# An interleaved attention and Fourier network on one core: when the output projection of the attention layers starts, and how its rows are spread over the steps

## The chip, the cores and the metric

The kernel runs on one core of a Trainium2 chip. The metric is the device time of one execution in microseconds. The core has a matrix engine (PE, with its weight loads PEld), a vector engine (DVE), a scalar engine (ACT), a general engine (POOL) and an engine that issues transfers (SP). Each works through its own instructions in order and waits on semaphores for the others.

## The reference

The input has 2048 rows of 640 numbers. Four layers follow each other: attention, Fourier, attention, Fourier. Each adds its result to its input. The change touches the attention layers alone.

```python
def _A_ref(x, wqkv, wo):
    B, S, D = x.shape
    H = 32; Dh = D // H; W = 256
    qkv = (lambda x, *d: x.transpose(*d))((x @ wqkv).reshape(B, S, 3, H, Dh), 2, 0, 3, 1, 4)
    q, k, v = qkv[0], qkv[1], qkv[2]
    scores = jnp.einsum("bhqd,bhkd->bhqk", q, k) * (Dh ** -0.5)
    idx = jnp.arange(S)
    mask = (idx[:, None] - idx[None, :] >= 0) & (idx[:, None] - idx[None, :] < W)
    scores = jnp.where(mask[None, None], scores, -1e9)
    p = _softmax(scores, axis=-1)
    o = jnp.einsum("bhqk,bhkd->bhqd", p, v)
    return (lambda x, *d: x.transpose(*d))(o, 0, 2, 1, 3).reshape(B, S, D) @ wo

def _B_ref(x, dft_seq_re, dft_seq_im, dft_hid_re, dft_hid_im):
    a = jnp.einsum("bsd,ed->bse", x, dft_hid_re)
    b = jnp.einsum("bsd,ed->bse", x, dft_hid_im)
    y = jnp.einsum("ts,bse->bte", dft_seq_re, a) - jnp.einsum("ts,bse->bte", dft_seq_im, b)
    return y

x = A_x
x = x + _A_ref(_layernorm(x, axis=-1), A_wqkv, A_wo)
x = x + _B_ref(_layernorm(x, axis=-1), B_dft_seq_re, B_dft_seq_im, B_dft_hid_re, B_dft_hid_im)
x = x + _A_ref(_layernorm(x, axis=-1), A_wqkv, A_wo)
x = x + _B_ref(_layernorm(x, axis=-1), B_dft_seq_re, B_dft_seq_im, B_dft_hid_re, B_dft_hid_im)
```

## The kernel before

Products that need full precision split each operand into a rounded high part and the rest (`split`, `cut_job`), and add three products, high by high, high by low and low by high.

**The heads.** An attention layer treats its 32 heads as 8 quads of four. A quad has 16 blocks of 128 rows, so `heads` walks through 128 steps. In step t PE computes the scores of one key block for four heads in two halves (`t_pair`, L657), ACT takes their exponential (`t_exp`, L667), POOL masks it (L673, L677), and one step later PE multiplies the probabilities with the values (`pv`, L692). Ten steps ahead, for unit s = t + 10, PE computes the same scores the other way round (`s_head`, L629), DVE adds a mask and takes the row maxima (L634). Every four steps the maxima are transposed (`m_rows`, L642), ACT writes them to the tile mt, and a transfer on SP (qp<-mt, L647) puts them into two rows of the query tile, where the scores of two to five blocks later need them. So the step t = 16 q + 2 needs the maxima that step t - 4 made.

**The fill.** Between the two halves of a step `fill` gives PE a few matmuls of other work. First this is the projection to queries and keys (`project`, `pieces`): ten chunks of 128 columns (c = 0 to 9, of which 2 to 9 are filled in), each over four quarters of the sequence (sb = 0 to 3), two quarters at a time. Two matmuls on 64 rows each run beside each other (`lockstep`, L255), first one half of the rows, then the other; such a piece pair has 60 matmuls and takes eight steps at the rate of four pairs a step. Its result goes through ACT and POOL to a tile c and with a transfer (qk_d<-c, L522) to memory. `pack` reads it back, for each quad and quarter in twelve transfers, three a step (qp<-qk_d, kp<-qk_d, L592). The list `due` tells at which s a quarter of a quad is packed and how much of the projection must be done by then.

**The output projection.** When the projection is through, `fill` goes on with `partials`: the 16 blocks of output rows, four to a quarter. The inner dimension of 640 is cut into five operand chunks that `CHUNKS` lists by heads: chunks 0 and 1 need heads 0 to 15 (quads 0 to 3), chunk 2 heads 16 to 23, chunk 3 heads 24 to 31, chunk 4 all. A row takes the chunks 0, 1 and 2 early (`EARLY` is 3), 36 matmuls of 64 by 320, with the residual input added on DVE (L975, `y_part`), and the chunks 3 and 4 late (`late`), 12 whole matmuls (L237), after the last heads. `load_y` loads the residual rows (big<-x, L949), four at once at the end of the projection and then one a row. `load_o` loads an operand chunk (x<-o_d, L857) and, once for chunks 0 and 1 together, the reciprocal sums (rr<-r_d, L863); POOL scales (L890), ACT and DVE cut. `prepare` loads and cuts the weights wo and starts the first operand set, at the last projection chunk. `LATE` is the number of matmul pairs in a fill of this phase: 9 for half a row, so a row takes two steps. `after_heads` does the last early rows, the late rows, and the first units of the Fourier layer (L1380).

In the timeline of before, step 92 starts at 413.15 us, step 97 at 426.39, step 98 at 431.97, step 99 at 436.86, step 118 at 500.77, step 125 at 521.74 and step 127 at 526.41; in the second attention layer step 97 starts at 1516.08.

## Time and profile before

| what | value |
|---|---|
| median of 3 runs | 2202.13 us (2198.74 to 2204.55) |
| profiled execution | 2201.15 us, span 2199.4 us |
| PE busy | 2127.3 us, 97% |
| DVE busy | 1620.9 us, 74% |
| ACT busy | 1139.1 us, 52% |
| POOL busy | 969.0 us, 44% |
| transfers | 392.09 MB, mean 178 GB/s |

Busy shares hide two things here. A matmul that waits inside PE's pipeline counts as busy, so the length of a step says more than its busy share. And the losses of one attention layer sit in some 110 us, the steps 92 to 127, and come twice. A view by stretches shows them. "PE banks L657 <- DMA qp<-mt" reads: PE's instruction of line 657, which writes the tile banks, waited for the landing of the transfer that writes qp from mt. Rows of SP give the time of an issue, not of a transfer.

### The profile page before, as it was taken

Reading aid. Unit: us, or ns where it says so; the run is one execution under the profiler, and the core shown is the slowest. Engines: PE = TensorE matmul, PEld = TensorE weight load, DVE = VectorE, ACT = ScalarE, POOL = GpSimd, SP = SyncE. Lnnn points to the kernel's source line nnn. Section 1 sums busy time; section 2 is a strip of 40 time slices with the busy share of each in tenths; the row PEclk is TensorE's granted clock in tenths of the full one; section 3 lists DMA queues with packets and bytes.
Section 4 is the critical chain, followed back from the end, with each engine's and each line's share of the span. In section 5 each row is a group of like instructions: output and inputs, shape, how many; then the busy total and the mean of one; then the engine's idle time right before and its main releaser. Section 6 shows DMA issues by size and latency. Waiting matters only on the chain.

```text
span 2199.4 us, 48840 instructions
## 1 busy us (share of the span) xinstructions
PE 2127.3 (97%) x17872; PEld 1785.7 (81%) x17872; DVE 1620.9 (74%) x3949; ACT 1139.1 (52%) x2125; POOL 969.0 (44%) x1568
## 2 busy tenths in 40 slices
PE   7999999998999999999999999999999999999999
PEld 7987777677868888889999777776777788888899
DVE  6358888786897868776661688887868968687776
ACT  3117776656554545552431377676655545455332
POOL 3037776765513223232330477677655133231324
PEclk9999999999999999999999999999999999999999
DMA  5556656785435453665646466668753354546643
GB/s 182 175 162 186 201 181 207 224 221 164 161 122 171 138 185 127 221 199 194 208 146 188 149 199 183 201 195 231 216 170 135 128 187 135 166 152 207 226 161 127
DMA packets 220175, 392.09 MB, mean 178 GB/s; under 512 B 39200, under 2 KB 85792, under 8 KB 219936
## 3 DMA queue, kind: packets, MB, share of 16 engines
q1 hardware_dynamic: 219936, 388.98, 56.4%
q8 instruction: 141, 2.31, 0.4%
q14 instruction: 98, 0.80, 0.1%
HBM read 273.94 MB, written 113.77 MB: 176 GB/s over the span
## 4 chain that ended last, share of the span: by engine, by line
PE 79%; DVE 7%; ACT 4%; DMA 4%; POOL 3%; issue 3%; SPq 0%; ACTq 0%; DVEq 0%; POOLq 0%
PE banks L1380 29%; PE banks L237 15%; PE banks L255 13%; PE banks L692 6%; PE banks L657 5%; PE banks L1668 5%; PE banks L629 4%; DVE banks L634 1%; DMA qp<-qk_d 1%; DVE qp L230 1%; ACT pt L667 1%; DMA qk_d<-c 1%; PE banks L339 1%; POOL rs L1084 1%; ACT big L1036 1%
## 5 line engine op out<-in xcount | busy, mean ns | idle before, releaser
L634 DVE CUSTOM_DVE_ANT_0 banks<-banks,mask 128x384 f32<-128x384 f32 (+2 forms) x1024 | 527.4, 557 | 120.2 <-PE banks L629 97.3
L667 ACT ACTIVATE pt<-banks 128x768 f32<-128x768 f32 (+2 forms) x512 | 393.7, 772 | 172.0 <-PE banks L657 66.4
L673 POOL TENSOR_SCALAR_AFFINE_SELECT pt<-pt 128x256 f32<-128x256 f32 x512 | 214.7, 420 | 217.5 <-ACT pt L667 197.8
L255 PE MATMUL banks<-big,wc 64*128 64x512 f32 x1920 | 270.8, 394 | 0.4 <-DVE pt L440 0.4
L657 PE MATMUL banks<-qp,kp 61*128 61x384 f32 (+2 forms) x1024 | 210.8, 382 | 24.8 <-DVE mc L634 17.6
L692 PE MATMUL banks<-pt,vq 128*32 128x128 f32 x5760 | 212.0, 278 | 3.5 <-ACT pt L667 3.5
L629 PE MATMUL banks<-kp,qp 60*128 60x384 f32 (+2 forms) x1024 | 205.6, 346 | 4.7 <-DVE mc L634 3.0
L255 PEld LDWEIGHTS banks<-big,wc 64*128 64x128 f32 x1920 | 185.7, 185 | 23.5 <-ACT x L542 1.5
L224 ACT ACTIVATE qp<-pt 128x512 fp32r<-128x512 f32 (+1 forms) x201 | 124.0, 625 | 140.2 <-DVE pt L1314 56.7
L677 POOL TENSOR_SCALAR_AFFINE_SELECT pt<-pt 128x256 f32<-128x256 f32 x448 | 194.0, 433 | 0.0
L692 PEld LDWEIGHTS banks<-pt,vq 128*32 128x32 f32 x5760 | 142.5, 110 | 51.4 <-issue 35.6
L230 DVE TENSOR_TENSOR qp<-pt,qp 128x512 fp32r<-128x512 f32 (+1 forms) x199 | 153.8, 781 | 41.0 <-ACT qp L224 39.3
L657 PEld LDWEIGHTS banks<-qp,kp 61*128 61x128 f32 x1024 | 108.6, 185 | 90.0 <-DVE mc L634 63.9
L1313 POOL TENSOR_TENSOR pt<-pt,pt 128x512 f32<-128x512 f32 x34 | 50.6, 1488 | 241.3 <-DMA pt<-c 166.4
L1380 PE MATMUL banks<-qp,big 128*128 128x512 f32 x648 | 154.5, 392 | 0.0
L224 ACT ACTIVATE c<-pt 128x512 fp32r<-128x512 f32 x144 | 89.3, 625 | 120.3 <-POOL pt L1300 56.4
L629 PEld LDWEIGHTS banks<-kp,qp 60*128 60x128 f32 x1024 | 123.8, 186 | 30.5 <-DVE mc L634 18.2
L634 DVE DVE_READ_ACCUMULATOR2_ANT mc<- 128x1 f32 x1024 | 145.0, 142 | 0.0
L1380 PEld LDWEIGHTS banks<-qp,big 128*128 128x128 f32 x648 | 121.5, 189 | 25.2 <-POOL qp L230 0.9
L230 DVE TENSOR_TENSOR c<-pt,c 128x512 fp32r<-128x512 f32 x142 | 113.9, 804 | 26.9 <-ACT c L224 24.3
L1380 PE MATMUL banks<-qp,xc 128*128 128x512 f32 x480 | 119.0, 394 | 6.5 <-DVE xc L230 3.7
L1380 PEld LDWEIGHTS banks<-qp,xc 128*128 128x128 f32 x480 | 90.2, 189 | 28.5 <-DVE xc L230 6.3
(248 smaller groups left out, 4464.5 us busy)
## 6 DMA issues: line engine op xcount, KB each, us to landing
pt<-c SPq DMA_DIRECT2D x188, 512.0 KB
qk_d<-c SPq DMA_DIRECT2D x80, 512.0 KB
kp<-qk_d SPq DMA_DIRECT2D x384, 80.0 KB
qp<-qk_d SPq DMA_DIRECT2D x384, 80.0 KB
kp<-u_d SPq DMA_DIRECT2D x32, 640.0 KB
o_d<-ou SPq DMA_DIRECT2D x64, 256.0 KB
x_d<-x SPq DMA_DIRECT2D x48, 320.0 KB
v_d<-pt SPq DMA_DIRECT2D x16, 768.0 KB
```

The costliest lines, as they stand in the source:

```text
L224: nc.scalar.activation(hi, src, AF.Copy, scale=-1.0 if neg else 1.0)
L230: (eng or nc.vector).tensor_tensor(out=lo, in0=src, in1=hi.bitcast(F32), op=OP.subtract)
L237: self.nc.tensor.matmul(p, x, y, start=n == 0, stop=n == last)
L255: self.nc.tensor.matmul(ps[a], x[r], y[r], start=half + i == 0, stop=half == 1 and i == n - 1, skip_group_check=True)
L629: nc.tensor.matmul(p, qp[quad % 2][b:b + 60, z, qb * P:(qb + 1) * P], kp[quad % 2][b:b + 60, z, k0 * P:(qb + 1) * P], start=True, stop=True)
L634: nc.vector.tensor_tensor_reduce(out=p, in0=p, in1=self.mask[:, 384 - n * P:], scale=1.0, scalar=NEG, op0=OP.add, op1=OP.max, accum_out=mc ...
L657: nc.tensor.matmul(self.banks[:, banks[e], :n * P], kp[quad % 2][b:b + 61, z, kb * P:(kb + 1) * P], qp[quad % 2][b:b + 61, z, kb * P:(kb + ...
L667: nc.scalar.activation(pt[quad, kb][:, 2 * z:2 * z + 2, :n * P], self.banks[:, b0:b1 + 1, :n * P], AF.Exp, scale=SCALE)
L673: nc.gpsimd.affine_select(out=t[:, :, 0:P], in_=t[:, :, 0:P], pattern=[[0, 2], [1, P]], compare_op=OP.is_ge, fill=0.0, base=0, channel_mul ...
L677: nc.gpsimd.affine_select(out=t[:, :, 256:384], in_=t[:, :, 256:384], pattern=[[0, 2], [-1, P]], compare_op=OP.is_gt, fill=0.0, base=0, ch ...
L692: nc.tensor.matmul(self.banks[32 * h:32 * h + 32, bank, :P], vq[:, 96 * (kb % 4) + 21 * h:96 * (kb % 4) + 21 * h + 32], t[:, h, (qb - kb) ...
L1380: nc.tensor.matmul(self.banks[:, bk, :], p, b[q], start=start and m == 0, stop=stop and last and m == 2, skip_group_check=True)
```

## The change

It does four things. (1) For the first four output rows (quarter 0) only the chunks 0 and 1 are early (`FEW` is 2) and three are late; chunk 2 of that quarter then gets its own place in the tile qp. (2) The chunks 8 and 9 of the projection are filled in by halves of the sequence: chunk 8 and then chunk 9 for the quarters 0 and 1, then both for 2 and 3 (`LAST`); the packs of the quarters 2 and 3 of quad 6 come two steps later. (3) `prepare` issues its loads one by one, some steps apart. (4) `LATE` depends on the half of a row and on the step: 9 pairs for the first half, and for the second 5 and 4 in two steps, so that a row of three chunks takes three steps; from s = 128 on (step 118) it is 9 and 9 as before. Each tile of reciprocal sums is now held by name until its last use (`rr_held`).

```diff
-LATE = 9
+LATE = (9, 5), (9, 9)
+FEW = 2
+LAST = [(c, sbs) for sbs in ((0, 1), (2, 3)) for c in (NCH - 2, NCH - 1)]
...
     def project(self):
-        for c in range(2, NCH):
+        for c in range(2, NCH - 2):
             lead = self.lead
...
-                if c == NCH - 1:
-                    self.prepare(sbs[0])
                 yield from self.pieces(c, sbs, "f" if lead else "m")
-        self.prepare(4)
+        for c, sbs in LAST:
+            if (c, sbs) == LAST[0]:
+                self.load_chunk(NCH - 1)
+                self.post(6, lambda: self.cut_chunk(NCH - 1))
+            if (c, sbs) == LAST[2]:
+                self.prepare()
+            yield from self.pieces(c, sbs, "m")
+        self.take_big(2, F32)
+        self.load_y(range(AHEAD_X))
...
-        due = [(16 * q + 4 * j - AHEAD, ((-(-160 * (q + 1) // P) - 1) * NSB + 2 * (j // 2) + 2) * per_piece)
+        due = [(16 * q + 4 * j - AHEAD + 2 * (q == NQ - 2 and j > 1), pos[-(-160 * (q + 1) // P) - 1, j // 2], q, j)
...
-                    size = -(-left // max(1, round(left / n)))
+                    size = -(-left // max(1, round(left / n[self.side])))
...
-                nf = LATE
+                nf = LATE[s >= steps]
...
+    def early_ks(self, sb):
+        return range(FEW if sb == 0 else EARLY)
+
+    def prepare(self):
...
+        for at, f, k in ((3, load, 0), (5, first, 0), (7, load, 1), (9, first, 1), (11, load, 2)):
+            self.post(at, lambda f=f, k=k: f(k))
...
     def late_set(self, sb):
-        ks = range(EARLY, KC)
-        return dict(zip(ks, pairs(cuts(self.kp[sb // 2][:, sb % 2 * 2048:(sb % 2 + 1) * 2048], 512))))
+        o = dict(zip(range(EARLY, KC), pairs(cuts(self.kp[sb // 2][:, sb % 2 * 2048:(sb % 2 + 1) * 2048], 512))))
+        if sb == 0:
+            o.update(zip(range(FEW, EARLY), pairs(cuts(self.qp[0][:, 4 * D:], 512))))
+        return o
+
+    def late_ks(self, sb):
+        return range(len(self.early_ks(sb)), KC)
...
-        w = dict(zip(ks, self.late_w))
+        w = dict(zip(range(KC), self.early_w + self.late_w))
```

**PE, step 92 of the first attention layer.** A step begins with the two matmuls of `t_pair` (L657 before, L669 after); L629 and L641 are `s_head`, L255 and L261 the fill, L692 and L704 `pv`. Tiles are named with the number of their buffer. Before:

```order
L657 MATMUL banks<-qp_104,kp_103 128x384 x2
L629 MATMUL banks<-kp_560,qp_105 128x384 x2
L657 MATMUL banks<-qp_104,kp_103 128x384 x2
L629 MATMUL banks<-kp_560,qp_105 128x384 x2
L692 MATMUL banks<-pt_95,vq_92 32x128 x4
L692 MATMUL banks<-pt_96,vq_92 32x128 x4
```

After, in the same step:

```order
L669 MATMUL banks<-qp_104,kp_103 128x384 x2
L641 MATMUL banks<-kp_560,qp_105 128x384 x2
L261 MATMUL banks<-big_5119,big_5120 128x320 x12
L669 MATMUL banks<-qp_104,kp_103 128x384 x2
L641 MATMUL banks<-kp_560,qp_105 128x384 x2
L704 MATMUL banks<-pt_95,vq_92 32x128 x4
```

The steps 92 to 96 had no fill. Now the first four rows stand there, 12 matmuls in each of the steps 92 to 99 where 18 stood in the steps from 97 on; step 100 has none.

**PE, steps 101 and 102 after.** Before, each of the steps 97 to 124 had 18 fill matmuls (`banks<-big_5481,big_5482 128x320 x18`). After:

```order
L669 MATMUL banks<-qp_105,kp_560 128x384 x2
L641 MATMUL banks<-kp_560,qp_105 128x384 x2
L261 MATMUL banks<-big_5119,big_5120 128x320 x12
L261 MATMUL banks<-big_5119 128x320 x6
L669 MATMUL banks<-qp_105,kp_560 128x384 x2
L641 MATMUL banks<-kp_560,qp_105 128x384 x2
L704 MATMUL banks<-pt_96,vq_91 32x128 x4
L704 MATMUL banks<-pt_97,vq_91 32x128 x4
L704 MATMUL banks<-pt_94,vq_92 32x128 x4
L669 MATMUL banks<-qp_105,kp_560 128x384 x2
L641 MATMUL banks<-kp_103,qp_104 128x128 x2
L261 MATMUL banks<-big_5119,big_5120 128x320 x10
```

A row of three chunks has 18 matmuls in its first step, 10 in its second and 8 in its third; so it goes on to step 118, and from 119 to 126 each step has 18. In all, 14 early rows stand in the steps up to 126, as many as before in the steps up to 124.

**SP, steps 92 to 94.** L619 loads values, L949 the residual rows, L592 is `pack` (qp_105 and kp_560 belong to quad 6, qp_104 and kp_103 to quad 7), L522 stores the projection, L709, L710 and L715 belong to the end of a quad's quarter, L647 moves the maxima that step 98 needs. Before:

```order
L619 DMA vq_91<-v_d 128x384
L949 DMA big_5879<-x 128x640 x4
L592 DMA qp_105<-qk_d 20x2x512 x3
L522 DMA qk_d<-c 128x2x512
L709 DMA sm<-ou_98 128x1x16
L710 DMA o_d<-ou_98 128x512
L715 DMA r_d<-rc 128x16
L592 DMA kp_103<-qk_d 20x2x512 x3
L522 DMA qk_d<-c 128x2x512
L647 DMA qp_105<-mt 2x4x128 x2
```

After (L631 is L619 of before, L967 is L949, L875 and L883 are L857 and L863, L604 is L592, L528 is L522, L721 to L727 are L709 to L715, L659 is L647), first up to the store of step 93:

```order
L631 DMA vq_91<-v_d 128x384
L967 DMA big_5871<-x 128x640 x5
L875 DMA x<-o_d 128x1x512
L883 DMA rr_100<-r_d 128x1x512
L875 DMA x<-o_d 128x1x512
L604 DMA kp_560<-qk_d 20x2x512 x3
L528 DMA qk_d<-c 128x2x512
```

and from the end of step 93 on:

```order
L604 DMA qp_105<-qk_d 20x2x512 x3
L604 DMA kp_103<-qk_d 20x2x512 x3
L967 DMA big_5871<-x 128x640
L528 DMA qk_d<-c 128x2x512
L875 DMA x<-o_d 128x1x512
L883 DMA rr_101<-r_d 128x1x512
L659 DMA qp_105<-mt 2x4x128 x2
L604 DMA qp_105<-qk_d 20x2x512 x3
```

Between the first residual row and the maxima there stand two residual rows, five operand loads and three pack transfers more than before, and three query transfers of quad 6 (the last row), which stood ahead of the store before, now stand behind the maxima.

**DVE, step 93 after.** L646 is the mask and maximum of `s_head`, L994 the sum of a row with its residual; before, the first such sum stood in step 98.

```order
L646 ISA banks,mc<-banks,mask 128x384
L646 ISA mc 128x1
L646 ISA banks,mc<-banks,mask 128x384
L646 ISA mc 128x1
L994 TENSOR_TENSOR big_5871<-banks,big_5871 128x640
L646 ISA banks,mc<-banks,mask 128x384
```

The sum of the first row stands one step behind the issue of its residual row, where it stood six steps behind it.

More of the change, by code (lines that the diff above doesn't have):

```diff
@@ L102, in __init__ @@
         self.heavy = []
-        self.left = 0
+        self.left, self.side = 0, 0
+        self.rr_held = {}
         self.tmp = None
@@ L247, in lockstep @@
         for half in range(2):
+            self.side = half
             for ps, terms in sets:
@@ L841, in load_o @@
         o["left"] = o.get("left", 0) + 1
-        if not self.after and not all((q, sb) in self.stored for q in range(h0 // 4, h1 // 4)):
+        shared = k and CHUNKS[k - 1][:2] == (h0, h1)
+        free = next((i for i in range(3) if i not in self.rr_held), None)
+        if (shared and ("rr", sb, k - 1) not in self.turn or rr is None and not shared and free is None) or not self.after and not all(
+                (q, sb) in self.stored for q in range(h0 // 4, h1 // 4)):
             def again():
@@ L857, in load_o @@
         nc.sync.dma_start(raw, src if nh >= nd else src.rearrange("h d s -> d h s"))
-        if k and CHUNKS[k - 1][:2] == (h0, h1):
-            rr = self.turn.pop(("rr", sb))
-        else:
-            rr = self.next("rr") if rr is None else rr
+        if shared:
+            rr = self.turn.pop(("rr", sb, k - 1))
+        else:
+            if rr is None:
+                rr = self.rr[free]
+                self.rr_held[free] = sb, k + (k + 1 < KC and CHUNKS[k + 1][:2] == (h0, h1))
             src = self.rd[sb, h0:h1, :]
@@ L953, in partials @@
         nc = self.nc
-        ks, w, sets = range(EARLY), self.early_w, self.early_o
+        w, sets = self.early_w, self.early_o
         self.take_big(3, F32)
@@ L998, in late_load @@
         rrs = (None, None, None, self.vq)[sb]
-        for k, r in zip(range(EARLY, KC), raws):
-            self.load_o(o, sb, k, r, rrs and rrs[k - EARLY])
+        for k in self.late_ks(sb):
+            if k < EARLY:
+                self.load_o(o, sb, k)
+            else:
+                self.load_o(o, sb, k, raws[k - EARLY], rrs and rrs[k - EARLY])
     def poll_late(self, n):
@@ L1031, in late @@
         self.flush("lw")
-        ks = range(EARLY, KC)
-        w = dict(zip(ks, self.late_w))
+        w = dict(zip(range(KC), self.early_w + self.late_w))
         def scaled(t, xw, st, nm, c0, c1):
```

60 lines of the change are left out of this document (28 added, 32 removed).

## The prediction

> **What bounds the kernel now.** I read the page for the span, then cut the part of the first attention layer that the change touches into stretches at the first matmul of a step (a step is one group of four L657 matmuls, 128 steps to a layer). The columns are the stretch, its length, busy us and count of PE, PEld, DVE, ACT and POOL, the granted clock, the DMA share and GB/s.
>
> ```profile
> span 2199.4 us, 48840 instructions
> core 0: us, PE busy (x) PEld busy (x) DVE busy (x) ACT busy (x) POOL busy (x), PEclk, DMA share, GB/s
> 357.40:389.71 32.31, 31.95 (x459) 24.61 (x455) 27.32 (x99) 22.85 (x43) 20.90 (x51) 1.00 0.64 196
> 413.15:426.39 13.24, 11.62 (x165) 7.46 (x161) 11.88 (x43) 8.67 (x19) 11.27 (x25) 1.00 0.83 261
> 426.39:436.86 10.47, 7.82 (x77) 5.68 (x77) 5.89 (x21) 3.80 (x6) 3.66 (x11) 0.85 0.70 200
> 436.86:500.77 63.91, 58.94 (x936) 49.20 (x932) 53.45 (x181) 38.84 (x70) 41.40 (x89) 1.00 0.78 211
> 500.77:521.74 20.97, 19.31 (x329) 15.81 (x325) 8.74 (x18) 15.68 (x30) 16.30 (x34) 1.00 0.53 157
> 521.74:526.41 4.67, 3.23 (x56) 1.98 (x56) 2.17 (x4) 3.54 (x7) 3.72 (x8) 0.94 0.51 141
> 526.41:541.80 15.39, 13.70 (x123) 12.46 (x119) 11.20 (x24) 7.46 (x16) 4.81 (x6) 0.91 0.51 159
> ...
> 1516.08:1526.69 10.61, 7.94 (x77) 6.08 (x78) 5.45 (x20) 3.80 (x6) 3.22 (x10) 0.84 0.78 214
> 1611.42:1616.51 5.09, 3.65 (x57) 2.34 (x58) 2.17 (x4) 3.54 (x7) 3.72 (x8) 0.82 0.52 173
> ```
>
> These are steps 72 to 83 (2.69 us a step, PE 99% busy), 92 to 96 (no fill, yet 2.65 us a step), 97 and 98, 99 to 117 (3.36 a step), 118 to 124 (3.00), 125 and 126 (no fill), and what follows. The two lowest rows are steps 97 to 98 and 125 to 126 of the second attention layer; they show the same losses, so I price one layer and double it. A step without fill is as long as one with eight fill matmuls, because DVE (11.88 of 13.24) paces it: five such steps waste PE time that rows could have used.
>
> Steps 97 and 98 take 10.47 us where two steps of the next stretch take 6.7. The timelines of PE and DVE and the chain of waits say why.
>
> ```profile
> 429.57 0.44 PE L629 MATMUL banks<-kp,qp 60*128 60x384 f32 x2 [1.04 <-DMA qp<-mt]
> 431.97 0.45 PE L657 MATMUL banks<-qp,kp 61*128 61x384 f32 x2 [1.60 <-DMA qp<-mt]
> ```
> ```profile
> 428.75 0.25 DVE L712 RECIPROCAL rc<-sm 128x16 f32<-128x16 f32 x1 [1.89 <-DMA sm<-ou]
> ```
> ```profile
> 420.99 7.56 DMA qk_d<-c
> ...
> 428.61 3.23 DMA qp<-mt
> ...
> 437.58 1.32 PE banks L255 x18
> ...
> 551.76 1.77 PE banks L237 x12
> ```
>
> Step 98 could not start before the row maxima (qp<-mt) had landed at 428.61 + 3.23 = 431.84. Their issue stood eight places behind the store qk_d<-c of 420.99, and that store landed at 428.55: SP keeps eight transfers in flight and waits for the oldest. So here the transfer queue, not PE, decides. The last two rows give prices: 0.073 us for a matmul of a row in halves (1.32 / 18), 0.147 us for a whole one (1.77 / 12).
>
> **The change, part by part, for one attention layer.**
>
> A. Steps 76 to 91. The same loads, cuts and scalings of the first operand set stand earlier and apart.
>
> ```profile
> L209 DVE TENSOR_TENSOR big<-we,big 128x640 fp32r<-128x640 f32 x2 | 2.0, 1017 | 0.0
> L890 POOL TENSOR_TENSOR x<-x,rr 128x256 f32<-128x256 f32 x24 | 18.0, 748 | 0.0
> ```
>
> Apart, the 1.02 us cuts no longer fall together; on the other hand POOL gets all its pieces of 0.75 us in steps 82 to 87, behind which it can fall back by a step. The cover is PE's eight fill matmuls in each of these steps; without it, a piece or two would show. I take 0, from -1.0 (one cut gained) to +1.5 (two POOL pieces shown).
>
> B. Steps 92 to 98. Two-chunk rows now fill steps 92 to 99, 12 matmuls each, 0.88 us, so by PE alone they would run like steps 72 to 83 (2.69) or a little longer for the sums on DVE, and step 98 would start near 413.15 + 6 x 2.8 = 430. But the queue gets more to do ahead of the maxima. The SP timeline of before, and the transfer view of 413 to 437 (forty slices of 0.6 us):
>
> ```profile
> 411.46 0.57 SPq L857 DMA_DIRECT2D x<-o_d  x1
> 412.68 0.55 SPq L863 DMA_DIRECT2D rr<-r_d  x1
> 413.33 1.17 SPq L647 DMA_DIRECT2D qp<-mt  x2
> ...
> 417.78 1.79 SPq L949 DMA_DIRECT2D big<-x  x4
> ...
> 422.18 0.61 SPq L709 DMA_DIRECT2D sm<-ou  x1
> ```
> ```profile
> GB/s 147 263 225 270 116 157 178 181 171 201 299 308 252 316 316 329 311 350 376 385 307 270 223 181 161 329 390 256 102 69 171 201 167 239 186 111 236 198 218 179
> ...
> big<-x SPq DMA_DIRECT2D x5, 320.0 KB
> qk_d<-c SPq DMA_DIRECT2D x2, 512.0 KB
> qp<-qk_d SPq DMA_DIRECT2D x12, 80.0 KB
> ...
> rr<-r_d SPq DMA_DIRECT2D x2, 256.0 KB
> x<-o_d SPq DMA_DIRECT2D x2, 256.0 KB
> o_d<-ou SPq DMA_DIRECT2D x1, 256.0 KB
> ```
>
> By the order, before passes from the first big<-x to the maxima 4 x 320 + 6 x 80 + 2 x 512 + 256 = 3040 KB. After passes 6 x 320 + 9 x 80 + 2 x 512 + 256 + 5 x 256 (three x<-o_d, two rr<-r_d) = 5200 KB, 2160 KB (2.21 MB) more. The ten fullest slices in a row (299 to 385) have a mean of 324 GB/s: 6.8 us. The two transfers of 411.46 and 412.68 are no longer in front, which gives back 413.33 - 411.46 = 1.9. The maxima land at 431.84 + 6.8 - 1.9 = 436.7. Behind them now stand the last three query pieces of the quarter that step 98 multiplies (240 KB, 0.7): step 98 is held to about 437.5, 5.5 later than now. It then takes what it took, less six matmuls (0.4) that it no longer holds; its slow clock, 0.85 in the row, stays. B = +5.1. Bounds: at 385 GB/s, +4.0; at 3040 KB in the 14.06 us from 417.78 to 431.84 (216 KB a us) and without the 1.9 given back, +10.3. I take the saturated rate since a queue that has more waiting stays saturated.
>
> In front of this another wait is new: DVE's sum of the first row, in step 93, needs the first big<-x. That took 4.3 us (the issue eight places on, at 422.18, had to wait for it), so from about 415.9 it lands at 420.2, while DVE gets there near 417. Behind it in DVE's order stand the mask operations of steps 93 on, whose banks PE waits for. Those 3 us lie inside the hold of step 98 and cost nothing more.
>
> The Trainium skill, page "DMA: Bandwidth & Descriptors", section "Specifications", gives about 358 GB/s as the limit of one core towards HBM. As an estimate from that page the 2.21 MB would take 6.2 us, and the sum would come out 1.2 us lower for both layers; the trace agrees for the mean of the ten slices, and two of them (376, 385) lie above it.
>
> C. Steps 99 to 126, now 63.91 + 20.97 + 4.67 = 89.55 us. After, step 99 has 12 fill matmuls, 100 none, 101 to 118 hold six rows at three steps each (18, 10 and 8), 119 to 126 four rows at two steps.
>
> ```profile
> L634 DVE CUSTOM_DVE_ANT_0 banks<-banks,mask 128x384 f32<-128x384 f32 x68 | 36.7, 581 | 5.1 <-PE banks L629 4.6
> L975 DVE TENSOR_TENSOR big<-banks,big 128x640 f32<-128x640 f32 x9 | 7.4, 825 | 2.9 <-PE banks L255 2.0 <-PE banks L657 1.0
> L209 DVE TENSOR_TENSOR big<-x,big 128x512 fp32r<-128x512 f32 x4 | 3.7, 916 | 0.0
> L261 DVE COPY seen<-banks 128x2 f32<-128x2 f32 x10 | 1.6, 159 | 2.0 <-PE banks L255 2.0
> ```
>
> PE's part of a step beside the fill is 58.94 / 19 - 1.32 = 1.78 us; 18 steps and 216 matmuls make 18 x 1.78 + 15.8 = 47.8. DVE: without rows and cuts (7.4 + 1.6 + 3.7) its 53.45 us are 2.14 a step; 18 x 2.14 + 6 x 0.98 + 4 x 0.92 = 48.1. The two are now even. Today 63.91 us hold 58.94 of PE, a ratio of 1.08; I take 1.09, 52.5 us (2.92 a step). Bounds: 1.01, the ratio of steps 72 to 83, 48.5; DVE's ratio today (63.91 / 53.45 = 1.20), 57.5. Step 99 is 2.8, step 100 is 2.65 like the unfilled ones, 119 to 126 are 8 x 3.00 = 24.0. Sum 82.0, C = -7.6 (-11.6 to -2.6). The operand loads of the second and third set stand five and four steps earlier than now, so no row waits for its cut.
>
> D. The clock at the end of the heads. Steps 125 and 126 have no fill today.
>
> ```profile
> 523.46 0.86 PE L692 MATMUL banks<-pt,vq 128*32 128x128 f32 x24 [1.07 <-ACT pt L667]
> ...
> 526.82 3.12 PE L237 MATMUL banks<-qp,kp 128*128 128x320 f32 x12
> ...
> 530.92 2.03 PE L237 MATMUL banks<-qp,kp 128*128 128x320 f32 x12
> ```
>
> The rows of the stretches show the clock at 0.94 and 0.91 (0.82 in the second layer), and the same twelve matmuls at 3.12 and at 2.03 us. After, steps 125 and 126 are filled and only 127 is not: D = -1.1, from -2.2 (both layers' clock, twice that) to 0.
>
> The Trainium skill, page "TensorE: Matmul & The Clock Gate", Part 1, lets the clock fall after an idle window of about 3.4 us; by that alone these steps, whose longest wait is 1.07 us, would keep their clock, D would be 0 and the sum 2.2 us higher. The trace does not agree (0.82 to 0.94), and the rows decide.
>
> E. After the heads. Four rows have six more whole matmuls each: 24 x 0.147 = 3.5 us.
>
> ```profile
> L237 PE MATMUL banks<-qp,kp 128*128 128x320 f32 x143 | 25.4, 328 | 4.5 <-DVE x L1075 1.8 <-DVE big L975 1.7 <-ACT big L224 1.0
> ```
>
> Between 526 and 580 these matmuls wait 4.5 us for DVE and ACT, which are behind with rows and cuts; longer rows give them time. I take 2.0 of it as cover, E = +1.5 (0 to +3.5). The two transfers more for the third chunk of these rows are issued at step 120, eight steps before the first such row; nothing is queued behind them.
>
> The sum is 0 + 5.1 - 7.6 - 1.1 + 1.5 = -2.1 a layer, -4.2 for two. The profiled execution took 2201.15 us (span 2199.4), 1 us under the median of 2202.13: 2197.
>
> **The rivals.** (1) The queue does not hold step 98: B is -1.5 (it starts at 430.5), the sum -8.7 a layer, 2184. For it: before 419 the slices show 116 to 270 GB/s, so there is room for what stands in front. Against it: SP issues in order and the added loads stand behind the queue's fullest place. (2) On the other side: the three-step rows are no faster a step than now, 3.36 us, since DVE, even with PE and waiting for a row's matmuls (2.9 + 2.0 us today), sets the step. Then 101 to 118 take 60.5, the sum is +5.9 a layer, 2213. It decides (slower by over 0.3%) from 58 us on, 3.2 a step. For it: DVE is busy 84% in rows of two steps and 90% in unfilled steps. Against it: steps 72 to 83 run at 2.69 with DVE at 85%. (3) The queue at its slow bound, B = +10.3: +3.1 a layer, 2207, no change that a measurement tells, and slower with any second loss.
>
> **How the numbers follow.** A measurement of this kernel cannot tell less than about 0.3% (6.6 us) from no change. The forecast and the milder half of rival 3 lie inside it: 0.38. Rival 1, or C near its lower bound: 0.35. Rival 2 and the rest of rival 3: 0.27. The half widths of A to E (1.2, 3.1, 4.5, 1.1, 1.8) combine as a root of squares to 6.0 a layer, 12 for two, and to reach rivals 1 and 2 the range goes from 2184 to 2212.
>
> **What would show it.** B: the maxima of step 98 landing 5 us later than now, counted from step 92, PE waiting there for qp<-mt or for qp<-qk_d, and a DVE sum in step 93 that waits for big<-x. C: 101 to 118 at 2.9 us a step, no step of over 4 us. D: no clock under 0.95 around step 126. E: the waits of L237 after the heads down by some 2 us. The forecast is wrong if step 98 starts within 2 us of now or more than 10 later, or if three-step rows run at 2.7 or 3.2 us a step.

## The result, and the profile after

The changed kernel takes 2216.1 us in the median of four runs (2215.2 to 2218.5), beside 2202.0 for the kernel before on the same chip. The ratio is 1.0069, with a 95% interval from 1.0056 to 1.0081: slower by 14 us, where 2197 and "no change" were forecast and the range ended at 2212.

The profiled execution has a span of 2214.6 us, 15.2 more than before. PE executes 48 instructions fewer (48 halves less and 24 whole matmuls more, in each of two layers) and is busy 5.5 us longer, 2132.8 against 2127.3 us:

```profile
span 2214.6 us, 48716 instructions
PE 2132.8 (96%) x17824; PEld 1793.7 (81%) x17824; DVE 1627.1 (73%) x3951; ACT 1137.7 (51%) x2125; POOL 963.9 (44%) x1564
```

The view by stretches, cut at the first matmul of a step (now L669) as before, with the same columns. The first six rows are steps 92 to 96, 97 and 98, 99 and 100, 101 to 118, 119 to 126, and 127 to the first Fourier unit of the first attention layer. The last three are steps 92 to 98, 101 to 118 and 119 to 126 of the second.

```profile
414.43:434.71 20.28, 16.14 (x226) 13.25 (x222) 13.05 (x47) 8.39 (x18) 10.61 (x24) 0.83 0.86 253
434.71:445.13 10.42, 7.59 (x69) 5.37 (x65) 6.49 (x22) 4.93 (x9) 6.75 (x15) 0.75 0.80 242
445.13:451.81 6.68, 5.67 (x81) 4.22 (x77) 5.32 (x17) 4.60 (x9) 4.58 (x11) 0.87 0.63 175
451.81:503.93 52.12, 49.94 (x770) 39.58 (x770) 44.94 (x160) 34.69 (x64) 33.60 (x77) 1.00 0.73 205
503.93:528.61 24.68, 21.78 (x372) 17.88 (x368) 10.96 (x19) 17.92 (x33) 18.39 (x39) 1.00 0.48 145
528.61:548.04 19.43, 18.64 (x165) 17.50 (x161) 13.67 (x34) 7.74 (x16) 5.45 (x7) 1.00 0.80 212
...
1512.02:1544.58 32.56, 22.87 (x291) 17.71 (x288) 19.56 (x68) 13.58 (x26) 17.34 (x38) 0.81 0.81 236
1551.09:1603.23 52.14, 49.93 (x769) 39.60 (x769) 44.94 (x160) 34.69 (x64) 33.58 (x77) 1.00 0.74 202
1603.23:1627.93 24.70, 22.07 (x372) 17.91 (x369) 10.41 (x19) 17.95 (x33) 18.41 (x39) 1.00 0.49 150
```

The steps 92 to 96 were to cost a little more than their 13.24 us and took 20.28; 97 and 98 still take 10.42, where 10.47 stood before, but 14.28 in the second layer, where 10.61 stood. The steps 101 to 118 came out as forecast, 52.1 us. The clock around step 126 is 1.00 now.

I cut both profiled executions at five marks; the table has the lengths in us, first / second attention layer. The last mark is the 300th matmul of the Fourier units (L1407, before L1380), well behind the last output row.

| stretch | term | before | after | difference | forecast |
|---|---|---|---|---|---|
| steps 76 to 91 | A | 44.9 / 45.0 | 45.7 / 45.7 | +0.8 / +0.7 | 0 |
| 92 to 98 | B | 23.7 / 24.0 | 30.7 / 32.6 | +7.0 / +8.6 | +5.1 |
| 99 to 126 | C | 89.6 / 89.8 | 83.5 / 83.4 | -6.1 / -6.5 | -7.6 |
| 127 to the 300th matmul | D and E | 120.9 / 122.1 | 127.7 / 127.3 | +6.8 / +5.2 | +0.4 |

These add up to +8.5 and +8.0 a layer, 16.5 for both; the rest of the span gives back 1.3. Against the forecast A is off by less than 1 us a layer, B by 1.9 and 3.5, C by 1.5 and 1.1, and the tail behind the heads by 6.4 and 4.8. Each stretch is read from one execution of each kernel.

From the timeline of PE the wait that opens step 94 and two waits in step 98, and from that of DVE the wait in step 93:

```profile
423.69 0.58 PE L669 MATMUL banks<-qp,kp 61*128 61x256 f32 x2 [3.75 <-DMA kp<-qk_d]
439.54 0.44 PE L669 MATMUL banks<-qp,kp 61*128 61x384 f32 x2 [2.28 <-DMA qp<-mt]
440.98 0.66 PE L641 MATMUL banks<-kp,qp 60*128 60x384 f32 x1 [0.56 <-DMA qp<-qk_d]
```
```profile
422.28 0.82 DVE L994 TENSOR_TENSOR big<-banks,big 128x640 f32<-128x640 f32 x1 [3.22 <-DMA big<-x]
```

The signs that the prediction named for B are there: step 98 starts 6.3 us later than before, counted from step 92 (25.1 instead of 18.8; 7.4 later in the second layer), it waits for its maxima and then for its query pieces, and the first sum waits 3.22 us for the first residual row. In the first line the name kp<-qk_d is doubtful: those transfers were issued from 422.47 on, and by their semaphores they land from 429 on. PE's instruction also waits for DVE, whose mask operation behind that sum ends at 423.6; in the second layer the profile names DVE at this place. So this is the wait for the residual row, passed on to PE.

Behind the heads, the groups of instructions (both layers together, before and after) and the timeline of PE in the first layer show this:

```profile
L237 PE MATMUL banks<-qp,kp 128*128 128x320 f32 x384 | 65.9, 322 | 8.0 <-DVE x L1075 3.5 <-ACT big L224 2.6 <-DVE big L975 1.7
```
```profile
L242 PE MATMUL banks<-qp,kp 128*128 128x320 f32 x384 | 64.9, 316 | 9.0 <-DVE x L1102 9.0
```
```profile
553.72 2.11 PE L1407 MATMUL banks<-qp,big 128*128 128x512 f32 x8 [1.46 <-DVE qp L235]
558.13 2.49 PE L242 MATMUL banks<-qp,kp 128*128 128x320 f32 x12 [2.31 <-DVE x L1102]
560.42 3.38 PE L1407 MATMUL banks<-qp,big 128*128 128x512 f32 x9
...
576.69 2.02 PE L242 MATMUL banks<-qp,kp 128*128 128x320 f32 x12 [1.43 <-DVE x L1102]
```

This group of the late rows' matmuls waited 8.0 us for DVE and ACT before, 4.5 in the first layer and 3.5 in the second, and now waits 9.0 us for DVE, 3.7 and 5.3. All waits of PE in the tail together went from 8.5 / 8.7 to 11.5 / 11.3 us. The forecast had these waits shrink by 2.0 a layer. After the wait at 558 nine matmuls of a unit take 3.38 us, where nine others at full clock take 2.23.

### The profile page after: what moved, and what is told of

Read it like the earlier page. It is cut to its first block, busy times and chain, and to the rows that moved or that the text cites. A ratio compares the mean times of both kernels' runs of the same rounds, so it can differ in the third digit from the quotient of the medians.

```text
span 2214.6 us, 48716 instructions
## 1 busy us (share of the span) xinstructions
PE 2132.8 (96%) x17824; PEld 1793.7 (81%) x17824; DVE 1627.1 (73%) x3951; ACT 1137.7 (51%) x2125; POOL 963.9 (44%) x1564
## 4 chain that ended last, share of the span: by engine, by line
PE 75%; DVE 8%; DMA 6%; ACT 4%; POOL 4%; issue 3%; SPq 1%; ACTq 0%; DVEq 0%; POOLq 0%
PE banks L1407 28%; PE banks L242 15%; PE banks L261 11%; PE banks L704 6%; PE banks L1695 5%; PE banks L669 5%; PE banks L641 4%; DMA rr<-r_d 1%; DMA qp<-qk_d 1%; DVE qp L235 1%; ACT pt L679 1%; DVE banks L646 1%; DMA x<-o_d 1%; POOL pt L685 1%; PE banks L345 1%
## 5 line engine op out<-in xcount | busy, mean ns | idle before, releaser
L646 DVE CUSTOM_DVE_ANT_0 banks<-banks,mask 128x384 f32<-128x384 f32 (+2 forms) x1024 | 527.4, 557 | 133.8 <-PE banks L641 111.0
L261 PE MATMUL banks<-big,wc 64*128 64x512 f32 x1920 | 271.6, 395 | 0.4 <-DVE pt L446 0.4
L669 PE MATMUL banks<-qp,kp 61*128 61x384 f32 (+2 forms) x1024 | 210.8, 382 | 30.1 <-DVE mc L646 13.3
L641 PE MATMUL banks<-kp,qp 60*128 60x384 f32 (+2 forms) x1024 | 213.3, 352 | 4.0 <-DMA qp<-qk_d 1.6
L704 PE MATMUL banks<-pt,vq 128*32 128x128 f32 x5760 | 212.5, 279 | 2.7 <-ACT pt L679 2.5
L261 PEld LDWEIGHTS banks<-big,wc 64*128 64x128 f32 x1920 | 187.2, 186 | 22.1 <-ACT x L548 1.7
L235 DVE TENSOR_TENSOR qp<-pt,qp 128x512 fp32r<-128x512 f32 (+1 forms) x199 | 158.8, 806 | 40.2 <-ACT qp L229 38.5
L669 PEld LDWEIGHTS banks<-qp,kp 61*128 61x128 f32 x1024 | 109.0, 186 | 93.4 <-DVE mc L646 63.0
L704 PEld LDWEIGHTS banks<-pt,vq 128*32 128x32 f32 x5760 | 142.9, 110 | 50.5 <-issue 36.2
L1407 PE MATMUL banks<-qp,big 128*128 128x512 f32 x648 | 155.5, 393 | 3.8 <-DVE qp L235 2.9
L641 PEld LDWEIGHTS banks<-kp,qp 60*128 60x128 f32 x1024 | 128.1, 188 | 31.8 <-DVE mc L646 11.6
L1407 PEld LDWEIGHTS banks<-qp,big 128*128 128x128 f32 x648 | 122.0, 190 | 29.5 <-DVE qp L235 3.6
L646 DVE DVE_READ_ACCUMULATOR2_ANT mc<- 128x1 f32 x1024 | 144.5, 141 | 0.0
L1407 PE MATMUL banks<-qp,xc 128*128 128x512 f32 x480 | 120.5, 398 | 6.9 <-DVE xc L235 4.1
L1407 PEld LDWEIGHTS banks<-qp,xc 128*128 128x128 f32 x480 | 91.2, 191 | 29.0 <-DVE xc L235 6.6
```

The source lines that it names most:

```text
L235: (eng or nc.vector).tensor_tensor(out=lo, in0=src, in1=hi.bitcast(F32), op=OP.subtract)
L261: self.nc.tensor.matmul(ps[a], x[r], y[r], start=half + i == 0, stop=half == 1 and i == n - 1, skip_group_check=True)
L641: nc.tensor.matmul(p, qp[quad % 2][b:b + 60, z, qb * P:(qb + 1) * P], kp[quad % 2][b:b + 60, z, k0 * P:(qb + 1) * P], start=True, stop=True)
L646: nc.vector.tensor_tensor_reduce(out=p, in0=p, in1=self.mask[:, 384 - n * P:], scale=1.0, scalar=NEG, op0=OP.add, op1=OP.max, accum_out=mc ...
L669: nc.tensor.matmul(self.banks[:, banks[e], :n * P], kp[quad % 2][b:b + 61, z, kb * P:(kb + 1) * P], qp[quad % 2][b:b + 61, z, kb * P:(kb + ...
L704: nc.tensor.matmul(self.banks[32 * h:32 * h + 32, bank, :P], vq[:, 96 * (kb % 4) + 21 * h:96 * (kb % 4) + 21 * h + 32], t[:, h, (qb - kb) ...
```

## The experiments

Each kernel is compared with the kernel before, run on the same chip. "Tail" is the last row of the table above. The theory after the result: the tail loses because 24 matmuls a layer are uncovered behind the heads and something more comes with them; the steps 92 to 98 lose because SP's transfers land late. The rivals: only order is lost in the tail; the pace of rows or the projection by halves is to blame; the maxima, not the bytes, hold step 98.

**The tail: without the third chunk's matmuls, and with the old order of units.** The first kernel leaves out 24 matmuls a layer and keeps all else:

```diff
-            ks = self.late_ks(sb)
+            ks = range(EARLY, KC)
```

> The changed kernel without the 24 whole matmuls a layer of the third operand chunk of the first four output rows (they are left out, their loads and cuts stay; the attention output of the first 512 rows lacks chunk 2). Tail theory, in its plain form: 24 x 0.147 = 3.5 us a layer are uncovered behind the heads, and nothing else is lost there: 2209. With the waits and the slow clock that come with them: 5 to 7 us a layer, 2202 to 2206. If only the order of rows and Fourier units costs, and the matmuls lie inside waits: 2214 to 2216.

Measured: 2203.0 us, ratio 1.0003 (0.9993 to 1.0014); the tail is 120.1 / 121.4 us, 0.7 to 0.8 under the kernel before. So it is the second answer: the 3.5 us of matmuls bring 2.4 to 4.1 us more a layer. PE's waits in this tail are 8.8 / 8.7 us, 2.7 and 2.6 less than in the changed kernel. The clock records of the traces hold full and half clock only, and the time at half clock is 3.4 / 6.2 us here, 6.8 / 6.8 in the changed kernel, worth at most half its length. The two together cover what the matmuls bring. The edit also changes more than I had meant. PE's order of work around the end of the heads (numbers are late rows, E14 and E15 the last two early rows, U a Fourier unit):

```
before:             0 1 | E14 E15 2 U 3 4 U 5 U ...
changed kernel:     0   | E14 E15 1 2 3 U 4 U 5 U ...
without the third:  0 1 | E14 E15 2 U 3 4 U 5 U ...
unit earlier:       0   | E14 E15 1 2 U 3 U 4 5 U ...
```

The heads take up to two late rows (`BACK`), and in the changed kernel two fills are left for them, both in step 128, the last pass, which only multiplies with the values. With `LATE` at 9 a late row of 12 matmuls comes out whole in one fill, one of 18 in two halves; so the changed kernel gets one row in, and three late rows follow one another behind the early ones. A unit may start when two rows are ready, so it comes a row later. Leaving out the matmuls undoes both. The second kernel (last line of the list) keeps the matmuls and lets the first unit start earlier:

```diff
-        if n > self.last_a2 or self.normed < self.need[n] + (n < self.last_a2 - 3):
+        if n > self.last_a2 or self.normed < self.need[n] + (0 < n < self.last_a2 - 3):
```

> The changed kernel, with the first Fourier unit allowed as soon as one row is ready (two before), so that it stands between the late rows 2 and 3, as in the kernel before; the other units move up behind it. Order theory: the late rows 1 to 3, now in a row, make PE wait for DVE by 1.4 and 2.3 us, and a unit of 9 matmuls (2.2 us) in their midst covers most of it: 2 to 4 us a layer, 2208 to 2212. Rival: the unit itself must wait for its operand, and the rows behind it with it: 2214 to 2220.

Measured: 2210.1 us, ratio 1.0046 (1.0029 to 1.0063), 5 to 6 us faster than the changed kernel, in the forecast range; the tail is 124.2 / 122.5, that is 3.5 and 4.7 less. The reason in the expectation is not what the waits of PE show for the first layer's tail (total us, times, longest), here of the changed kernel and then of this one:

```profile
PE banks L242 <- DVE x L1102: 3.7, 2, 2.3
PE banks L1407 <- DVE qp L235: 2.1, 2, 1.5
```
```profile
PE banks L242 <- DVE x L1102: 4.0, 2, 2.7
...
PE banks L1407 <- DVE qp L235: 0.6, 1, 0.6
```

The late rows wait for DVE as long as they did. What went are 1.5 us of a unit's own wait for its operand. All waits of PE in the tail fell by 1.5 and 1.6 us, to 10.0 / 9.7, and the time at half clock went from 6.8 / 6.8 us to 3.4 / 0, worth 1.7 and 3.4; the two add up to the gain within 0.3 us. The gain also varies: over the five kernels here that have this edit, ten layers, the tail is 124.7 us in the mean (122.5 to 127.1); over the changed kernel and the three below that have its rows and its order behind the heads (maxima on ACT, `AHEAD_X` of 2, the old pace), eight layers, it is 127.1 (125.9 to 128.9). The order is worth 2.4 us a layer by these, 4.1 by the pair above.

**The steps 92 to 98: where the bytes stand.** First the maxima were taken off SP:

```diff
-                self.post(1, lambda z=z: nc.sync.dma_start(
+                self.post(1, lambda z=z: nc.scalar.dma_start(
```

> The changed kernel, with the transfers of the row maxima (qp<-mt) issued by ACT instead of SP. Everything else as in the changed kernel (2216 us). If the queue on SP is what holds step 98 (the queue theory), the maxima land some 7 us earlier, but the three query pieces that step 98 also needs still stand on SP behind the operand loads and land where they do now, at most 1.5 us after the maxima; so step 98 starts 0 to 1.5 us earlier a layer, PE's wait there changes its name from qp<-mt to qp<-qk_d, and the time is 2213 to 2216 us. If the maxima alone hold it, step 98 starts 5 us earlier a layer: 2206. If the queue is not what costs there: 2216 and the same wait.

Measured: 2312.3 us, ratio 1.0513 (1.0497 to 1.0528), far from all three numbers. The timeline and the waits show another cost, all over the heads:

```profile
304.55 0.25 ACT L657 ACTIVATE mt<-banks 16x128 fp32r<-16x128 f32 x1
304.83 1.07 ACTq L659 DMA_DIRECT2D qp<-mt  x2
```
```profile
PE banks L641 <- ACT pt L679: 56.9, 61, 4.1
```

Two issues of 4 KB hold ACT for 1.07 us, in front of the exponential that PE's next scores wait for: 61 waits for 64 groups of maxima, and 96 us / 64 = 1.5 us a group. ACT is busy 49% of the span and has no slack at this place. On the question itself: PE's wait in step 98 became one of 4.8 us for qp<-qk_d, so the query pieces alone hold the step too.

Then the loads of the second operand set were put behind the maxima:

```diff
-                for k in range(2):
-                    self.load_o(sets[(sb + 1) % 2], sb + 1, k)
+                    def second():
+                        for k in range(2):
+                            self.load_o(sets[1], 1, k)
+                    self.post(6, second)
...
+                def third():
+                    self.load_o(sets[1], 1, 2)
+                self.post(6, third)
```

> The changed kernel, with the operand loads of the second set (three x<-o_d and two rr<-r_d of 256 KB, 1.28 MB a layer) issued three steps later, behind the maxima. Queue theory: 1.31 million bytes at 324 GB/s (the mean of the ten fullest slices of before) are 4.0 us; maxima and query pieces of step 98 land that much earlier, so 8 us for both layers: 2208 (2205 to 2211). Rival: the second set is now late and the row at step 101 waits for its cut, or the wait only moves to the next transfer: 2214 to 2220.

Measured: 2221.3 us, ratio 1.0099 (1.0082 to 1.0115). The steps 92 to 98 became shorter, 28.5 / 28.5 us, by 2.2 and 4.0; but the row of step 101 slipped to 103, as the rival said, the steps 99 to 126 took 85.2 / 85.8 instead of 83.5 / 83.4, the early rows of the heads end a step later, and the tail grew to 128.0 / 131.1. The set has no three steps to give.

The residual rows can be moved back with less risk:

```diff
-AHEAD_X = 4
+AHEAD_X = 2
```

> The changed kernel with AHEAD_X = 2 instead of 4: the residual rows are loaded two rows ahead, so two of the six big<-x of 320 KB that stood in front of the maxima stand behind them. Queue theory: 655 KB at 324 GB/s, 2.0 us earlier for the key pieces that step 93 waits for and for the maxima and query pieces of step 98, 4 us for both layers: 2212 (2210 to 2214). If step 98 is held by what SP issues at which time, and not by what lies in front: 2216. If the residual rows come late for DVE's sums: over 2218.

Measured: 2210.1 us, ratio 1.0041 (1.0025 to 1.0058), 6 us faster than the changed kernel where 4 was worked out. The steps 92 to 98 took 28.6 / 28.8 us, 2.1 and 3.8 less, where the bytes were to give 2.0. In the first layer DVE's wait for the first residual row went from 3.22 to 1.93 us, and PE's for the maxima stayed, in a step 98 that starts 2.4 us earlier after step 92; in the second layer the wait for the maxima went from 5.52 to 2.60 us:

```profile
421.12 0.82 DVE L994 TENSOR_TENSOR big<-banks,big 128x640 f32<-128x640 f32 x1 [1.93 <-DMA big<-x]
```
```profile
437.29 0.69 PE L669 MATMUL banks<-qp,kp 61*128 61x384 f32 x2 [2.06 <-DMA qp<-mt]
```

The next run joins the two edits, `AHEAD_X` and the earlier unit.

> The changed kernel with AHEAD_X = 2 and with the first Fourier unit allowed as soon as one row is ready (which alone gave 2210). The two lie 100 us apart, so their gains add: 2206 (2204 to 2209). If the gain of the queue is eaten by a later wait of the same layer: 2210.

Measured: 2207.5 us, ratio 1.0028 (1.0014 to 1.0042). By the ratios this is 9 us of the 11 that the two gave apart (5 and 6). In the profiled execution the first layer's tail has none of the order's gain (127.1 us), with a clock of 0.86 behind the first unit. One operand load is then moved as well:

```diff
-            if sb + 1 < NSB and i == 0:
+            if t == 0:
+                def third():
+                    self.load_o(sets[1], 1, 2)
+                self.post(2, third)
+            elif sb + 1 < NSB and i == 0:
                 self.load_o(sets[(sb + 1) % 2], sb + 1, 2)
```

> As the run before, and the third chunk's loads of the second operand set (one x<-o_d and one rr<-r_d, 512 KB a layer) are posted one step later, behind the maxima. Queue theory: 524 KB at 324 GB/s, 1.6 us a layer more: 2203 (2200 to 2206), if the set is still ready for its row at step 101. If that row slips, as it did with the whole set three steps later: 2209 or more.

Measured: 2206.6 us, ratio 1.0019 (1.0004 to 1.0033). Against the run before that is 0.9 us, within the uncertainty. The row of step 101 did not slip, and the steps 92 to 98 did not get shorter (29.5 / 30.0): inconclusive.

**Order or bandwidth.** The residual rows were then issued by POOL:

```diff
-                self.nc.sync.dma_start(self.y_part(t), self.xsrc[t * P:(t + 1) * P, :])
+                (self.nc.gpsimd if t < AHEAD_X + 2 else self.nc.sync).dma_start(
+                    self.y_part(t), self.xsrc[t * P:(t + 1) * P, :])
```

> The kernel with the first Fourier unit earlier (2210 us; AHEAD_X is 4 as in the changed kernel), with the first six residual rows of a layer (big<-x, 320 KB each) issued by POOL instead of SP. The bytes are the same, only the place in SP's order and among its eight transfers in flight is given free. If order is what holds step 98: 1.97 million bytes less ahead of the maxima on SP, 4 to 6 us a layer, 2198 to 2202. If it is the bandwidth that all share: 0 to 1 us a layer, 2208 to 2210. If the six issues hold up the masks on POOL, for which PE waits in turn: 2212 or more.

Measured: 2210.2 us, ratio 1.0051 (1.0033 to 1.0068), the same as with them on SP. The transfer view of 413 to 437 us:

```profile
q1 hardware_dynamic: 2771, 4.36, 58.1%
q0 software_dynamic: 480, 1.97, 26.6%
...
big<-x POOLq DMA_DIRECT2D x6, 320.0 KB, 7.0
```

SP's place in the order was free, but POOL's 1.97 MB run on the same sixteen engines, and by their semaphores eight of SP's transfers that met them took some 8.5 to 10 us, where those of the changed kernel took at most 7.2. POOL itself was held 2.88 us by the first five issues; what that costs was not separated. The steps 92 to 98 took 29.9 / 29.8 us, 1.0 and 2.8 less than with the rows on SP; of the 4 to 6 us that the order alone would have given, little is there. The Trainium skill, page "DMA: Bandwidth & Descriptors", section "Issuing engines are not separate DMA queues", says just this: transfers run on the same 16 engines whoever starts them, and several issuing engines only save the time of issuing. The run agrees (58.1% and 26.6% of the same engines).

On top of it, the maxima of one step alone:

```diff
-                self.post(1, lambda z=z: nc.sync.dma_start(
+                self.post(1, lambda z=z: (nc.scalar if (quad, u) == (NQ - 2, 1) else nc.sync).dma_start(
```

> As the run before, and the two transfers of the maxima that step 98 needs, those alone, are issued by ACT. With all maxima on ACT a group of two cost 1.5 us (96 us for 64 groups); here it is one group a layer, so at most 3 us. If step 98 then still waits for maxima on SP, this takes 2 us a layer away: 1 us faster than the run before; if the query pieces on SP come last, as with all maxima on ACT: up to 3 us slower than the run before.

Measured: 2214.1 us, ratio 1.0066 (1.0040 to 1.0091), 4 us over the run before, whose interval it overlaps. The profiled execution is the slowest of its four. The wait moved as the last line of the expectation has it:

```profile
438.50 0.44 PE L669 MATMUL banks<-qp,kp 61*128 61x384 f32 x2 [0.93 <-DVE mc L646]
445.49 0.66 PE L641 MATMUL banks<-kp,qp 60*128 60x384 f32 x1 [6.16 <-DMA qp<-qk_d]
```

In these runs no single transfer holds step 98: with the maxima out of SP's queue the query pieces do, and with the residual rows out of it both still come late.

**The other parts: the pace, and the projection by halves.**

```diff
-LATE = (9, 5), (9, 9)
+LATE = (9, 9), (9, 9)
```

> The changed kernel with the old pace: LATE is 9 and 9 everywhere, so the ten rows of three chunks take two steps each (101 to 120) and the steps 121 to 126 have no fill. In the changed kernel the steps 101 to 126 took 52.1 + 24.7 = 76.8 us in the first layer. If rows in two steps cost what they cost before, 20 x 3.36 + 6 x 2.65 = 83.1, 6.3 us a layer more: 2229 us. If the pace itself is worth nothing, since the same matmuls stand in the heads either way: 2216 to 2218.

Measured: 2223.7 us, ratio 1.0106 (1.0083 to 1.0128), 7.5 us slower than the changed kernel: the pace is worth 3.8 us a layer, between the two numbers. The stretches 101 to 118 and 119 to 126 of this run:

```profile
452.38:512.16 59.78, 55.39 (x878) 46.07 (x879) 49.98 (x169) 36.91 (x67) 38.85 (x84) 1.00 0.72 199
512.16:533.46 21.30, 17.66 (x265) 11.89 (x262) 7.48 (x13) 15.90 (x29) 13.73 (x32) 0.83 0.40 122
```

Rows in two steps cost 3.32 us a step, as before (3.36), and the stretch with six steps without fill falls to a clock of 0.83 in this layer (steps 99 to 126: 4.4 us more than in the changed kernel; in the second layer, with no such fall, 2.9 more). The rival that three-step rows would be no faster is refuted here a second time.

Without the moved rows and without the pace, the rest of the change stands alone:

```diff
-FEW = 2
+FEW = 3
-LATE = (9, 5), (9, 9)
+LATE = (9, 9), (9, 9)
...
-        for at, f, k in ((3, load, 0), (5, first, 0), (7, load, 1), (9, first, 1), (11, load, 2)):
+        for at, f, k in ((3, load, 0), (5, first, 0), (7, load, 1), (9, first, 1), (11, load, 2), (13, first, 2)):
```

> The changed kernel with FEW = 3 and LATE 9 and 9: of the change only the projection by halves of the sequence, the loads of prepare one by one and the named tiles of reciprocal sums are left; rows, their pace and the late chunks are as before. If these parts cost nothing: 2202 us (2199 to 2205). If they carry a part of the loss (step 92 starts 0.8 us a layer later in the changed kernel, and the packs of quad 6 stand two steps later in the queue): 2205 to 2210.

Measured: 2205.9 us, ratio 1.0027 (1.0013 to 1.0041). About 6 us (3 to 9) of the loss belong to the projection by halves and the loads of `prepare`, before any row is moved. The profiled execution, the slowest of the ten (2211.7 us), shows most of it in the steps 92 to 98, 28.9 / 26.4 us against 23.7 / 24.0; the query pieces of quad 6 now stand behind the maxima, and step 98 waits for both:

```profile
435.02 0.69 PE L669 MATMUL banks<-qp,kp 61*128 61x384 f32 x2 [2.56 <-DMA qp<-mt]
436.94 0.66 PE L641 MATMUL banks<-kp,qp 60*128 60x384 f32 x1 [0.94 <-DMA qp<-qk_d]
```

The stretch of steps 97 and 98 in this run, at a clock of 0.66:

```profile
426.67:441.86 15.19, 9.15 (x78) 6.64 (x78) 5.96 (x21) 3.80 (x6) 3.61 (x11) 0.66 0.77 216
```

**The queue in the kernel before.** If bytes ahead of the maxima cost time, the kernel before should gain from the same small edit, since four residual rows stand there too:

```diff
-AHEAD_X = 4
+AHEAD_X = 2
```

> The kernel before, with AHEAD_X = 2 and nothing else: two of the four residual rows that stood in front of the maxima of step 98 stand behind them. Queue theory: 655 KB at 324 GB/s are 2.0 us; step 98 waits 1.6 us for its maxima and step 97 1.0 us for its own pieces, so 1.6 to 2.6 us a layer go, up to the 2.0: 2197 to 2199 where the kernel before has 2201, a gain of 0.1 to 0.2%. If steps 97 and 98 are then held by something else (DVE, or the last pack of quad 7): 2201.

Measured: 2193.9 us in the median of 12 runs, ratio 0.9967 (0.9954 to 0.9980): faster than both kernels, and 7 us (4 to 10) faster than the kernel before, where 2 to 4 were forecast. In the first layer the mechanism is as worked out. The maxima land 2.4 us earlier (429.4 instead of 431.8), the wait of step 98 goes from 1.60 to 0.75, and with it the slow clock: steps 97 and 98 take 7.08 us at 1.00 instead of 10.47 at 0.85.

```profile
429.53 0.45 PE L657 MATMUL banks<-qp,kp 61*128 61x384 f32 x2 [0.75 <-DMA qp<-mt]
```
```profile
426.11:433.19 7.08, 6.02 (x79) 4.80 (x79) 5.56 (x20) 3.94 (x8) 3.36 (x10) 1.00 0.71 225
...
1512.36:1523.66 11.30, 7.69 (x78) 6.29 (x78) 5.45 (x20) 3.94 (x7) 3.24 (x10) 0.85 0.81 231
```

In the second layer it is not (last row: 11.30 us, before 10.61). There the profiled execution gained 3.4 us behind the heads, with the same order of instructions, at a higher clock. The whole execution spends 6.8 us at half clock instead of 23.9, worth at most 8.5 us, where its span is 7.9 shorter; over all runs the mean granted clock is 0.9963 instead of 0.9945, which is 4 of the 7 us. So the queue is shown for 3.4 us in the first layer; why the clock fell less often elsewhere stays open.

## Why the prediction was wrong

**E is the step that failed.** It read: four rows have six more whole matmuls each, 24 x 0.147 = 3.5 us, of which 2.0 are covered by waits for DVE and ACT; +1.5, at most +3.5. Without these matmuls and with the order before, the tail is 0.7 to 0.8 us under the kernel before, which is what D gives (forecast 1.1). So E is 127.7 - 120.1 = 7.6 and 127.3 - 121.4 = 5.9 us, above its own upper bound. Two things were missing. Nothing was covered: the waits of PE behind the heads did not shrink by 2.0 us but grew by 2.7 and 2.6 (from 8.8 / 8.7 without these matmuls to 11.5 / 11.3). DVE, for which the late rows wait, is busy 107.8 us of this tail in the first layer, 103.5 before, so longer rows gave it no time to catch up; that this is the reason is argued and was not tested by itself. And the order of rows and units changed, which costs 2.4 to 4.1 us: a row of 18 matmuls does not come out of one fill. The order of the changed kernel's instructions shows that; the prediction looks at it in the heads only. Of the 4.1 in the pair of kernels, some 1.5 are waits and 2.6 the clock.

**B was right in kind and too small.** The new waits came where they were said to be. Measured +7.0 / +8.6 instead of +5.1, within the bounds (+4.0 to +10.3): step 98 starts 6.3 and 7.4 us later where 5.5 were forecast, and is itself 0.7 and 1.2 us longer where 0.4 less were. That DVE's wait in step 93 lies inside the hold of step 98 is not refuted: ACT has the maxima in mt at 429.3 us, SP issues their transfer at 434.5, and PE still waits 2.28 us for it. I left the clock as it was, for steps 97 and 98 alone; it is 0.83 in the steps 92 to 96 and 0.75 in 97 and 98. A part, 5.2 and 2.4 us in the slowest of ten executions, is there already with the projection by halves alone; I had priced its part in the queue at 0.7 a layer.

**C was right in its main row** (52.1 us for 101 to 118, forecast 52.5), and 1.1 to 1.5 us too good a layer: step 99 took 3.7 us instead of 2.8, and 119 to 126 took 24.7 instead of 24.0. The gain needs both parts of it. With the matmuls moved out but the old pace it is 1.7 and 3.6 instead of 6.1 and 6.5.

**A** was +0.8 / +0.7, inside its bounds. **D** came as forecast: no clock under 0.95 around step 126. Over the whole tail of the changed kernel little is left of it, since the clock falls at other places: 6.3 / 8.4 us at half clock before, 6.8 / 6.8 after.

Rival 2 had 2213 us, near the time that was measured, and it is wrong: its three-step rows ran at 2.90 us a step. The range, which was to reach the rivals, ended 1 us below this one. The span came out 19.4 us over the forecast for both layers; 11.2 of them lie in the tail and 5.4 in B. The time lay outside the range because E was bounded by its matmuls and the order behind the heads was in no term.

## What to carry to other kernels

When work is moved over a boundary that a scheduler draws, compare the order on the far side too: a quota that a unit of work fitted whole may no longer fit it, and everything behind shifts by one. Waits seen in a profile are not free cover for more work on the waiting engine, if the engine waited for is the busy one. A few KB on which the next step depends want few bytes in front of them, on whatever queue; loading the residual rows two ahead instead of four was the one edit here that came out faster than the kernel before, though the queue explains only a part of it.

## What the hardware showed that I had not expected

Issuing is not free on an engine that sits in the critical chain. Two issues on ACT took 1.07 us, and cost 1.5 us a group with ACT at half load.

The clock values between 0.5 and 1 in the rows above are means. The clock records hold full and half clock only, and half comes in spells of 3.41 us or two to four times that, but for the last one at the program's end. In each trace all spells start on one beat of 3.41 us. Around one of them, in steps 97 to 100 of the kernel before, three pieces of this beat, with the columns of the stretches above:

```profile
430.29:433.70 3.41, 1.80 (x19) 1.41 (x17) 1.83 (x7) 1.09 (x2) 0.26 (x2) 1.00 0.56 165
433.70:437.11 3.41, 3.41 (x34) 2.33 (x32) 2.07 (x7) 0.92 (x2) 1.29 (x4) 0.50 0.89 192
437.11:440.52 3.41, 3.41 (x56) 2.95 (x58) 2.44 (x9) 2.21 (x5) 1.19 (x4) 1.00 1.05 265
```

PE was busy 1.80 us of the piece ahead of the spell. Over the fourteen executions kept here, without their first 60 and last 20 us, 104 such spells begin; PE was busy at most 60% of the 3.41 us ahead of 97 of them, but of only 54 of some 8600 pieces at full clock, and no piece with under 45% was followed by one at full clock. So a removed wait can save a whole spell, up to 1.7 us, beyond its own length, or none. The kernel before spends 23.9 us at half clock and the changed one 41.0, so at most 8.5 of the 15.2 us between their spans can be the clock.

A fall needs no long wait. In steps 97 and 98 of the first layer the clock stayed at 1.00 with a longest wait of 0.75 us, was 0.85 with 1.60, 0.75 with 2.28 and 0.66 with 2.56, but 0.71 with 6.16. The Trainium skill, page "TensorE: Matmul & The Clock Gate", Part 1, puts the fall after an idle window of about 3.4 us; three of these falls came with shorter waits, so the traces here do not agree with it as a rule for one wait.

The eight transfers in flight that the prediction reads come from this program: SP's 1874 transfers take eight completion semaphores in turn, and no issue in the two traces starts before the transfer eight places ahead of it has landed. Whether the chip has such a limit too, no run here shows.
